# Weight and form preparation in program order, other PSUM banks for the second layer, and another buffer for the transposed tokens

## The chip, the cores and the metric

The kernel runs on one core of a Trainium2 chip. TensorE (PE) multiplies, the vector engine (DVE), ScalarE (ACT) and GpSimd (POOL) work on the elements, and SyncE (SP) and POOL issue DMAs. Matrix results land in PSUM, which has eight banks; everything else lies in SBUF. The metric is the time of one execution on the device, in microseconds, lower is better.

## What is computed

Three layers follow one another on 2304 tokens (4 sequences of 576) of width 512; the reference, shortened:

```python
# 1: attention, 8 heads of 64, causal by blocks of 64
attn = softmax(mask(q @ k.T / 8)) @ v
x = attn.transpose(0, 2, 1, 3).reshape(2304, 512)
# 2: mixture of 8 experts, every token through every expert
P = exp(x @ w_gate - max)
for _ in range(8):
    P /= P.sum(1, keepdims=True); P /= P.sum(0, keepdims=True); P *= N / E
for e in range(8):
    out += P[:, e:e+1] * (relu(x @ w1[e]) @ w2[e])      # w1[e] 512x1024, w2[e] 1024x512
# 3: soft mixture, 8 experts of 4 slots
logits = out @ phi                                       # 2304 x 32
slot_in = softmax(logits, over tokens).T @ out           # 32 x 512
slot_out[e] = relu(slot_in[e] @ m2w1[e]) @ m2w2[e]
result = softmax(logits, over slots) @ slot_out
```

## The kernel before

Every float32 number of the second layer is held as a sum of two rounded halves, high and low, and a product is three matmuls: high x high, high x low, low x high. Products of 2x2 blocks are done with seven block products instead of eight, so there are sums and differences of blocks ("forms") on both sides: of the tokens (T1 to T4, B11, B21, B22), of the first weights (A11, A12, A22, S1 to S4) and of the second ones (B.., T..).

**The main loop** has 13 steps. A step takes two quarters of an expert's 1024 hidden columns ("a" and "b", 256 each) through all tokens, which are three chunks of 768, c = 0, 1, 2. For each chunk there is a first layer (`l1_steps`, matmuls at L880 into banks La, Lb, Lc; ACT copies and relus at L893, L904; DVE additions at L901 and combinations at L898, L912, L953; the splits of the hidden blocks into halves, high on ACT at L908 and low on DVE or POOL at L909) and a second layer (`L2S`, matmuls at L996 into banks l2a and l2c, three token tiles i = 0, 1, 2 at a time, added with the gate's weight into `acc` by DVE at L1003). L1ORD lists the first layer's pieces: the last matmuls are those of product 4, and then come the combinations of quarter a (`af ag ah ai`) and b (`bf bg bh bi`), which read the banks La for the last time. PMAJ lists the second layer: products P1 and P2 for the three tiles, and then the others.

**Preparation.** While a chunk runs, the weights of the next step are prepared, one item at a time: a form (`lin`, POOL, L785), its rounded high half (`hi`, ACT, L790) and the rest (`lo`, DVE, L794), from a raw tile `r` that a DMA has brought (`raw`). `pipe` staggers the three over successive calls, and `pops` and `pop2` call one after each piece of a layer. The ten early items of the first weights (W1E) are called in c = 2's first layer, the four late ones (W1L) in its second; the eight early ones of the second weights (W2E) in c = 0's first layer, the six late ones (W2L) in its second. The forms of the tokens (`forms`, L715 to L723) are built once, ahead of the main loop, in scratch tiles tA and tB.

**The order** on each engine is not the order of these calls. A scheduler lists the instructions by its own estimate of when they can run, and may put a preparation ahead of work that was written before it; each engine then goes through its list strictly in order.

**The last stage.** The last two quarters of the last expert run outside the loop (`L1BE`, `LMAJ`). As tokens are finished, the third layer begins: groups g of four tiles of 128 tokens are transposed (xt, L1185), copied by ACT into a buffer x2a (L1189), multiplied by phi (lg, L1197), and each group is closed with maximum, exponential, two transposes (dT, dR) and a product with the tokens (si, L1243). After the last group comes sit (L1361), and then the slots' two layers (h, sox, soy), whose weights `mw` SP loads in 128 pieces of 256 KB (L1151, L1155). x2a lies in the tile tagged `t4`, which is also the first layer's temporary t (L953).

## Time and profile before

| | us |
|---|---|
| median of three runs (lowest, highest) | 1929.01 (1927.41, 1934.23) |
| the profiled execution | 1932.13 |
| its span | 1930.2 |

Of that span attention and the first expert quarters take the first 450 us, the main loop runs to about 1715, the last quarters to 1832, and the slots' layers from 1870 to the end. PE is the busiest engine. In the profile an engine's row says when an instruction starts, how long it takes and, in brackets, how long the engine stood idle before it and what released it. Matmuls overlap, so that the spacing of their starts, and not their length, is what one costs. PEclk is the clock granted to PE as a share of 2.4 GHz; the other level is 1.2 GHz.

### The profile page before, as it was taken

The numbers are of one execution on the slowest core, as the hardware profiler recorded it, in microseconds if no ns is written. First come the engines' busy times: TensorE is split into PE (matmuls) and PEld (weight loads), VectorE is DVE, ScalarE is ACT, GpSimd is POOL, SyncE is SP. The second block draws the span as 40 slices with busy tenths as digits, with TensorE's granted clock in tenths as the row PEclk, the third lists the DMA queues.
The fourth block names the chain that finished last, engine by engine and source line by source line (L and its number), as shares of the span: only waits on it lengthen the run. The fifth ranks groups of instructions, "written<-read, shape, count | busy, mean of one in ns | idle before, by whom it ended". The sixth has DMA issues, their size and how long they took to land.

```text
span 1930.2 us, 33537 instructions
## 1 busy us (share of the span) xinstructions
PE 1807.6 (94%) x12109; PEld 1662.4 (86%) x12109; DVE 1394.3 (72%) x3154; ACT 908.4 (47%) x2260; POOL 786.1 (41%) x1068
## 2 busy tenths in 40 slices
PE   6999999889999999999999999999999999989987
PEld 4777788778899999999999999898999999989743
DVE  7877767597777777777777787878787878775511
ACT  5667646444535444444454545444444444442313
POOL 6535333444343434343435353535353535342110
PEclk9999999999999999999999999999999999999979
DMA  5544443685746464646464656565655555554759
GB/s 188 168 151 144 135 134 98 198 286 165 223 154 230 156 229 154 225 163 224 164 221 167 215 173 208 180 200 188 191 197 192 196 184 204 178 191 137 248 200 327
DMA packets 145204, 365.98 MB, mean 190 GB/s; under 512 B 12688, under 2 KB 82064, under 8 KB 145040
## 3 DMA queue, kind: packets, MB, share of 16 engines
q0 software_dynamic: 42336, 231.23, 35.7%
q1 hardware_dynamic: 102704, 132.62, 21.1%
q8 instruction: 96, 1.57, 0.3%
q14 instruction: 68, 0.56, 0.1%
HBM read 337.85 MB, written 25.95 MB: 188 GB/s over the span
## 4 chain that ended last, share of the span: by engine, by line
PE 53%; DVE 26%; ACT 8%; DMA 8%; issue 3%; POOL 2%; SPq 0%; ACTq 0%; POOLq 0%; DVEq 0%
PE l2a L996 12%; PE l2c L996 11%; PE La L880 7%; DMA r<-in_moe_w_dram 7%; PE Lb L880 6%; DVE w2f L794 4%; PE l L194 3%; ACT Hxl L893 3%; DVE tA L912 3%; DVE t L953 2%; DVE Hxl L898 2%; DVE tB L912 2%; PE pvp L542 2%; DVE tB L901 2%; DVE Hxh L909 2%
## 5 line engine op out<-in xcount | busy, mean ns | idle before, releaser
L880 PE MATMUL La<-XBT,w1f 128*128 128x384 f32 x1512 | 295.9, 339 | 4.4 <-DVE tB L901 4.4
L1003 DVE SCALAR_TENSOR_TENSOR acc<-l2a,P,acc 128x256 f32<-128x256 f32 x504 | 228.7, 477 | 75.1 <-PE l2a L996 74.6
L996 PE MATMUL l2a<-w2f,Hxl 128*128 128x256 f32 x1512 | 228.6, 288 | 49.4 <-ACT Hxl L908 42.6
L880 PEld LDWEIGHTS La<-XBT,w1f 128*128 128x128 f32 x1512 | 265.5, 188 | 8.7 <-DVE tB L901 8.6
L996 PEld LDWEIGHTS l2a<-w2f,Hxl 128*128 128x128 f32 x1512 | 205.3, 194 | 54.3 <-ACT Hxl L908 46.7
L1003 DVE SCALAR_TENSOR_TENSOR acc<-l2c,P,acc 128x256 f32<-128x256 f32 x378 | 168.4, 478 | 71.1 <-PE l2c L996 68.3
L996 PE MATMUL l2a<-w2f,Hxh 128*128 128x256 f32 x1134 | 191.5, 288 | 0.0
L996 PEld LDWEIGHTS l2a<-w2f,Hxh 128*128 128x128 f32 x1134 | 162.6, 196 | 1.1 <-issue 1.0
L996 PE MATMUL l2c<-w2f,Hxl 128*128 128x256 f32 x756 | 113.0, 297 | 10.8 <-DVE tB L912 10.8
L996 PEld LDWEIGHTS l2c<-w2f,Hxl 128*128 128x128 f32 x756 | 104.1, 203 | 19.2 <-DVE tB L912 19.2
L880 PE MATMUL Lb<-XBT,w1f 128*128 128x384 f32 x504 | 119.9, 360 | 0.0
L785 POOL TENSOR_TENSOR st<-r 128x256 f32<-128x256 f32 x112 | 86.0, 772 | 78.5 <-DMA r<-in_moe_w_dram 45.9
L790 ACT ACTIVATE w1f<-st 128x256 fp32r<-128x256 f32 x112 | 46.2, 413 | 141.0 <-PE Lb L880 119.9
L880 PE MATMUL La<-XBB,w1f 128*128 128x384 f32 x504 | 108.0, 346 | 2.3 <-DVE acc L1003 0.9
L880 PE MATMUL Lb<-XBB,w1f 128*128 128x384 f32 x504 | 102.8, 339 | 0.0
L880 PE MATMUL Lc<-XBB,w1f 128*128 128x384 f32 x504 | 102.5, 338 | 0.0
L996 PE MATMUL l2c<-w2f,Hhx 128*128 128x256 f32 x756 | 96.1, 280 | 0.0
L880 PEld LDWEIGHTS Lb<-XBT,w1f 128*128 128x128 f32 x504 | 95.9, 205 | 0.1
L489 POOL TENSOR_SCALAR pe<-pe,sm 128x384 f32<-128x384 f32 (+2 forms) x80 | 59.3, 744 | 84.2 <-DVE sm L476 43.0
L996 PEld LDWEIGHTS l2c<-w2f,Hhx 128*128 128x128 f32 x756 | 91.7, 188 | 0.8 <-issue 0.8
L880 PEld LDWEIGHTS La<-XBB,w1f 128*128 128x128 f32 x504 | 86.6, 192 | 6.2 <-DVE tA L912 4.5
L909 POOL TENSOR_TENSOR Hhx<-tA,Hhx 128x384 fp32r<-128x384 f32 x42 | 43.1, 1026 | 117.7 <-ACT Hhx L908 117.7
(275 smaller groups left out, 4508.1 us busy)
## 6 DMA issues: line engine op xcount, KB each, us to landing
XBT<-xf0T POOLq DMA_DIRECT2D x56, 768.0 KB, 5.8
XBT<-xf1T POOLq DMA_DIRECT2D x56, 768.0 KB, 7.0
XBT<-xf2T POOLq DMA_DIRECT2D x56, 768.0 KB, 6.1
r<-in_moe_w_dram SPq DMA_DIRECT2D x80, 512.0 KB, 5.9
mw<-in_moe_w_dram SPq DMA_DIRECT2D x128, 256.0 KB, 5.5
XBB<-xf0B POOLq DMA_DIRECT2D x42, 768.0 KB, 6.1
XBB<-xf1B POOLq DMA_DIRECT2D x42, 768.0 KB, 6.9
XBB<-xf2B POOLq DMA_DIRECT2D x42, 768.0 KB, 6.0
```

What stands on the lines that cost most here:

```text
L194: nc.tensor.matmul(o, lh, w[:, kf, :], start=(m == 0), stop=(m == 5))
L489: nc.gpsimd.tensor_scalar(out=p_[:, 0:n_], in0=p_[:, 0:n_], scalar1=sm[:, i:i + 1], scalar2=1.0, op0=ALU.mult, op1=ALU.mult)
L542: nc.tensor.matmul(o[64 * a:64 * a + 64, lo:hi], w, r(a), start=(m == 0), stop=(m == len(its) - 1))
L785: nc.gpsimd.tensor_tensor(out=o, in0=a, in1=b, op=alu)
L790: nc.scalar.activation(out=h, in_=src(), func=AF.Copy)
L794: nc.vector.tensor_tensor(out=lo, in0=src(), in1=f32(h), op=ALU.subtract)
L880: nc.tensor.matmul(o, w[:, i, k], x[:, j, k], start=(first and k == 0 and m == 0), stop=(k == 1 and m == 2), skip_group_check=not first)
L893: nc.scalar.activation(out=o, in_=i, func=AF.Relu)
L909: SLO[nm].tensor_tensor(out=h[:, 1], in0=t, in1=f32(h[:, 0]), op=ALU.subtract)
L912: nc.vector.scalar_tensor_tensor(out=o, in0=a, scalar=0.0, in1=b, op0=ALU.max, op1=op)
L996: nc.tensor.matmul(o, lh, rh, start=(m == 0 and p in ("P1", "P2", "P5")), stop=(m == 5), skip_group_check=p in ("P6", "P3", "P7", "P4"))
L1003: nc.vector.scalar_tensor_tensor(out=av, in0=o, scalar=P[:, t, e:e + 1], in1=av, op0=ALU.mult, op1=ALU.add)
```

## The change

1. `kp` keeps the preparation in the order in which it is written, on POOL, ACT and DVE, for forms and weights alike. `pipe` staggers by one call more (`lo` three calls after `lin`); two loads of the token forms come a call later, and so does the gate's maximum.
2. The late first-weight items and the raw loads of the second weights stand in another order.
3. In the second layer the banks of l2c are (7, 5, 3) instead of (3, 5, 4), and (4, 5, 3) in the last stage.
4. In the last stage c = 0's second layer is written ahead of the third layer's tiles; x2a lies in a free half of the tile H4 instead of `t4`, which becomes a second buffer for the last second layer only.

```diff
--- before.py
+++ after.py
@@ -246,7 +246,7 @@
                 side.append([gate_a(c)])
                 side.append([gate_b(c)] + ([gmax_a] if c == 2 * NCH - 1 else []))
                 if c == 2 * NCH - 1:
-                    side.append([gmax_b])
+                    side.extend([[], [gmax_b]])
                     for r in range(8):
                         side.extend([[] for _ in range(SG)])
                         side.append([col_norm(r == 7)])
@@ -681,16 +681,19 @@
     nst = [0]
     fdn = set()
 
+    def kp(ins):
+        tc.keep_in_program_order(ins)
+
     def pipe(items):
         n = len(items)
 
         def step(t):
             def f():
-                for j, m in ((t - 2, 2), (t - 1, 1), (t, 0)):
+                for j, m in ((t - 3, 2), (t - 2, 1), (t, 0)):
                     if 0 <= j < n and items[j][m] is not None:
                         items[j][m]()
             return f
-        return [step(t) for t in range(n + 2)]
+        return [step(t) for t in range(n + 3)]
 
     SG_T = ["w1f4", "w1f5", "w1f6"]
 
@@ -712,15 +715,15 @@
 
             def lin():
                 q = tmp4(k)
-                nc.gpsimd.tensor_tensor(out=q[o], in0=q[a], in1=q[b], op=alu)
+                kp(nc.gpsimd.tensor_tensor(out=q[o], in0=q[a], in1=q[b], op=alu))
 
             def hi():
                 st[0] = pb.tile([128, 2, HT], F32R, tag=SG_T[nst[0] % 3], name="stg")
                 nst[0] += 1
-                nc.scalar.activation(out=st[0][:, 0], in_=tmp4(k)[o], func=AF.Copy)
+                kp(nc.scalar.activation(out=st[0][:, 0], in_=tmp4(k)[o], func=AF.Copy))
 
             def lo():
-                nc.vector.tensor_tensor(out=st[0][:, 1], in0=tmp4(k)[o], in1=f32(st[0][:, 0]), op=ALU.subtract)
+                kp(nc.vector.tensor_tensor(out=st[0][:, 1], in0=tmp4(k)[o], in1=f32(st[0][:, 0]), op=ALU.subtract))
                 nc.sync.dma_start(out=xf[c, n][:, :, k, :], in_=f32(st[0]))
             return lin, hi, lo
 
@@ -782,16 +785,16 @@
         return st_t[ui][:, 0:256], st_t[ui][:, 256:512]
 
     def pop_(o, a, b, alu):
-        nc.gpsimd.tensor_tensor(out=o, in0=a, in1=b, op=alu)
+        kp(nc.gpsimd.tensor_tensor(out=o, in0=a, in1=b, op=alu))
 
     def prep(dst, src, lin):
         def hi():
             h, lo = dst()
-            nc.scalar.activation(out=h, in_=src(), func=AF.Copy)
+            kp(nc.scalar.activation(out=h, in_=src(), func=AF.Copy))
 
         def lo_():
             h, lo = dst()
-            nc.vector.tensor_tensor(out=lo, in0=src(), in1=f32(h), op=ALU.subtract)
+            kp(nc.vector.tensor_tensor(out=lo, in0=src(), in1=f32(h), op=ALU.subtract))
         return lin, hi, lo_
 
     def items_w1(u, ui):
@@ -847,7 +850,7 @@
         return [it["ab".index(x[0])][x[1:]] for x in names.split()]
 
     W1E = "aA11 aS1 bA11 aS2 bS1 aS4 bS2 aS3 bS4 bS3"
-    W1L = "aA12 bA12 aA22 bA22"
+    W1L = "aA12 aA22 bA12 bA22"
     W2E = "aB11 aT1 bB11 bT1 aB21 aT2 bB21 bT2"
     W2L = "aB22 bB22 aT4 bT4 aT3 bT3"
 
@@ -976,9 +979,9 @@
                 yield o
 
     SEQ = [("P1", "A11", "B11"), ("P2", "A12", "B21"), ("P5", "S1", "T1"), ("P6", "S2", "T2"), ("P3", "S4", "B22"), ("P7", "S3", "T3"), ("P4", "A22", "T4")]
-    ABK, CBK = (2, 1, 0), (3, 5, 4)
-
-    def L2S(c, e, order):
+    ABK, CBK, CBE = (2, 1, 0), (7, 5, 3), (4, 5, 3)
+
+    def L2S(c, e, order, cbk=CBK):
         oa, ob = {}, {}
 
         def prod(p, i, uis):
@@ -986,7 +989,7 @@
             if p == "P1" and 0 in uis:
                 oa[i] = bk(ABK[i], "l2a")[:, 0:256]
             if p in ("P2", "P5") and 0 in uis:
-                ob[i] = bk(CBK[i], "l2c")[:, 0:256]
+                ob[i] = bk(cbk[i], "l2c")[:, 0:256]
             o = ob[i] if p in ("P2", "P5", "P3") else oa[i]
             for ui in uis:
                 m = 3 * ui
@@ -1034,8 +1037,8 @@
         p = list(fo[c][2])
         if c + 1 < NCH:
             nb_, nl = fo[c + 1][0:2]
-            p[6] = lambda f=p[6]: (f(), nl(0))
-            p[9] = lambda f=p[9]: (f(), nl(1), nb_())
+            p[7] = lambda f=p[7]: (f(), nl(0))
+            p[10] = lambda f=p[10]: (f(), nl(1), nb_())
         return p
 
     p1 = fsteps(1)
@@ -1115,7 +1118,9 @@
             if c == 0:
                 l = (pipe(pick(items_w2, u0, W2L)) if s else []) + [raw(1, u0 + 2, 0), raw(1, u0 + 3, 1)]
             elif c == NCH - 1:
-                l = pipe(pick(items_w1, u0 + 2, W1L)) + [raw(2, u0 + 2, 0), raw(2, u0 + 3, 1)]
+                l = pipe(pick(items_w1, u0 + 2, W1L))
+                l[5:5] = [raw(2, u0 + 2, 0)]
+                l.append(raw(2, u0 + 3, 1))
             else:
                 l = []
 
@@ -1131,6 +1136,14 @@
     aux.extend([None] * 4 + pipe(pick(items_w2, u0, W2E)))
     l1_run(L1BE, lambda n: load_x(1, n), lambda j: pops(1))
     drain()
+    l = pipe(pick(items_w2, u0, W2L))
+
+    def pop2(j, x):
+        if j >= 6 and not (6 <= j < 18 and j % 2 == 0) and l:
+            run1(l.pop(0))
+    l2_run(L2S(0, e, PMAL, CBE), pop2)
+    while l:
+        run1(l.pop(0))
     ORD = list(range(12)) + [12, 15, 13, 16, 14, 17]
     wt, wtag = {}, []
     nload = [0]
@@ -1155,7 +1168,6 @@
                     nc.sync.dma_start(out=w[:, i].rearrange("p (k f) -> p k f", k=2), in_=m2w2[e_, r0:r0 + 256, 256 * xy:256 * xy + 256].rearrange("(k p) f -> p k f", p=128))
 
     cc = pb.tile([128, 512], F32, tag="cc", name="cc")
-    x2s = [pb.tile([128, 512], F32, tag="t4", name="x2a")]
     same, mb = cc[:, 0:128], cc[:, 256:384]
     phi_sb = cc[:, 128:256].rearrange("p (k s) -> p k s", k=KD)
     nc.sync.dma_start(out=same, in_=cst[:, 128:256])
@@ -1170,6 +1182,7 @@
     m18 = LVT[:, 968:968 + NT]
     H4 = pb.tile([128, 1024], F32, tag="r2", name="H4")
     nmask = H4[:, 512:640]
+    x2s = [H4[:, 0:512]]
     nc.gpsimd.tensor_scalar(out=nmask, in0=same, scalar1=-1.0, scalar2=-NEG, op0=ALU.add, op1=ALU.mult)
     mo = {}
     nx2 = [0]
@@ -1294,21 +1307,15 @@
         if last:
             load_w([(pb, f"w1f{i}", 2) for i in range(7)] + [(pb, "tB", 3), (pb, "tA0", 1), (pb, "tA1", 1)])
 
-            for p, i in L2S(c, e, [x for x in LMAJ]):
+            x2s.append(pb.tile([128, 512], F32, tag="t4", name="x2a"))
+            for p, i in L2S(c, e, LMAJ, CBE):
                 mpop()
                 if p == "P4":
                     push_t(3 if i < 2 else 4, (2 * i, 2 * i + 1) if i < 2 else (0, 1))
                     if i:
                         push_g(2 + i)
-        else:
-            l = pipe(pick(items_w2, u0, W2L)) if c == 0 else []
-
-            def pop2(j, x):
-                mpop()
-                if j >= 6 and not (6 <= j < 18 and j % 2 == 0) and l:
-                    run1(l.pop(0))
-            l2_run(L2S(c, e, PMAL), pop2)
-            assert not l
+        elif c:
+            l2_run(L2S(c, e, PMAL, CBE), lambda j, x: mpop())
         if c == 0:
             push_t(0, range(4))
             push_g(0)
```

Lines behind the first hunks move down by three (L790 is L793, L794 is L797, L908 is L911), those of the last stage by 13 (L1197 is L1210).

On ACT, around the transition of c = 2 in the first step. Before, with w2f a second-weight tile, Hxh, Hxl and Hhx hidden blocks, r_7740 the raw tile:

```order
L790 ACTIVATE w1f_5724<-st 128x256
L908 ACTIVATE Hxh_5940<-t_4947 128x384
L908 ACTIVATE Hxh_5955<-tB 128x384
L908 ACTIVATE Hhx_5944<-tA_4948 128x384
L790 ACTIVATE w2f_5738<-r_7740 128x256
L908 ACTIVATE Hxh_5955<-tB 128x384
L908 ACTIVATE Hxh_5940<-tA_4949 128x384
L908 ACTIVATE Hxl_5959<-t_4947 128x384
```

The same place now:

```order
L911 ACTIVATE Hxh_5955<-tB 128x384
L793 ACTIVATE w1f_5725<-st 128x256
L911 ACTIVATE Hxh_5940<-t_4947 128x384
L911 ACTIVATE Hxh_5955<-tB 128x384
L911 ACTIVATE Hhx_5944<-tA_4948 128x384
L911 ACTIVATE Hxl_5959<-t_4947 128x384
L911 ACTIVATE Hxh_5940<-tA_4949 128x384
L911 ACTIVATE Hhx_5963<-tB 128x384
L911 ACTIVATE Hxl_5959<-tB 128x384
L793 ACTIVATE w1f_5208<-r_7111 128x256
```

The second-weight item that stood among the splits is gone from here (it comes after the next chunk's first evictions); a first-weight item stands between the first two splits.

On DVE, the end of c = 0's first layer in the second step; L901 (now L904) adds a bank to a tile, L912 (L915) combines, L909 (L912) is a low half, L794 (L797) a preparation. Before:

```order
L953 TENSOR_TENSOR t_4947<-tA_4949 128x384
L909 TENSOR_TENSOR Hhl<-tA_4949,Hhl 128x384
L901 TENSOR_TENSOR tB<-Lc,tB 128x384
L909 TENSOR_TENSOR Hxh_5940<-t_4947,Hxh_5940 128x384
L912 SCALAR_TENSOR_TENSOR tA_4948<-tA_4948,t_4947 128x384
L912 SCALAR_TENSOR_TENSOR tB<-La,tB 128x384
L912 SCALAR_TENSOR_TENSOR tA_4949<-La,tA_4949 128x384
L953 TENSOR_TENSOR t_4947<-tB 128x384
L909 TENSOR_TENSOR Hxh_5955<-tB,Hxh_5955 128x384
L912 SCALAR_TENSOR_TENSOR tB<-tB,t_4947 128x384
L909 TENSOR_TENSOR Hxl_5959<-t_4947,Hxl_5959 128x384
L912 SCALAR_TENSOR_TENSOR tB<-La,tB 128x384
```

And now:

```order
L912 TENSOR_TENSOR Hhl<-tA_4949,Hhl 128x384
L904 TENSOR_TENSOR tB<-Lc,tB 128x384
L797 TENSOR_TENSOR w2f_5739<-r_7730,w2f_5739 128x256
L797 TENSOR_TENSOR w2f_5735<-st,w2f_5735 128x256
L956 TENSOR_TENSOR t_4947<-tA_4949 128x384
L915 SCALAR_TENSOR_TENSOR tB<-La,tB 128x384
L915 SCALAR_TENSOR_TENSOR tA_4948<-tA_4948,t_4947 128x384
L912 TENSOR_TENSOR Hxh_5940<-t_4947,Hxh_5940 128x384
L797 TENSOR_TENSOR w2f_5761<-r_7756,w2f_5761 128x256
L912 TENSOR_TENSOR Hxh_5955<-tB,Hxh_5955 128x384
L956 TENSOR_TENSOR t_4947<-tB 128x384
L915 SCALAR_TENSOR_TENSOR tA_4949<-La,tA_4949 128x384
```

The chain of combinations is the same; three preparations now stand in it, which before were ahead of the first layer's first addition.

On PE, the end of the last second layer (l2a, l2c) with the token steps (xt, lg). Before:

```order
L996 MATMUL l2a<-w2f_5750,Hhh 128x256 x3
L996 MATMUL l2a<-w2f_5772,Hxh_5955 128x256 x3
L1197 MATMUL lg<-x2a,cc 32x128 x4
L1185 MATMUL xt<-ident,acc_2939 128x128 x4
L1197 MATMUL lg<-x2a,cc 32x128 x4
L1185 MATMUL xt<-ident,acc_4145 128x128 x4
L1197 MATMUL lg<-x2a,cc 32x128 x4
L1185 MATMUL xt<-ident,acc_4145 128x128 x4
L1197 MATMUL lg<-x2a,cc 32x128 x4
L1226 MATMUL dT<-ident,LVT 128x128
L1243 MATMUL si<-acc_2939,LVT 32x512 x2
L1243 MATMUL si<-acc_4145,LVT 32x512 x2
```

And now:

```order
L1210 MATMUL lg<-x2a,cc 32x128 x4
L999 MATMUL l2a<-w2f_5747,Hxh_5940 128x256 x3
L999 MATMUL l2a<-w2f_5769,Hxl_5959 128x256 x3
L1198 MATMUL xt<-ident,acc_4908 128x128 x4
L1346 MATMUL mt<-H_19071,ident 128x128
L999 MATMUL l2a<-w2f_5751,Hhh 128x256 x3
L999 MATMUL l2a<-w2f_5773,Hxh_5955 128x256 x3
L1210 MATMUL lg<-H_19071,cc 32x128 x4
L1198 MATMUL xt<-ident,acc_4909 128x128 x4
L1239 MATMUL dT<-ident,H_19071 128x128
L1210 MATMUL lg<-x2a,cc 32x128 x4
L1256 MATMUL si<-acc_4907,LVT 32x512
```

Before, the last second-layer matmuls are followed by ten lg and eight xt of 4 matmuls each, of which the rows show the first ones; now by two lg and one xt.

## Rows read from the trace of the kernel before

**Rows 1.** The page: busy time, share and instructions by engine

```profile
PE 1807.6 (94%) x12109; PEld 1662.4 (86%) x12109; DVE 1394.3 (72%) x3154; ACT 908.4 (47%) x2260; POOL 786.1 (41%) x1068
```

**Rows 2.** PE's waits: what waited for what, us in total, times, longest

```profile
PE l2a L996 <- ACT Hxl L908: 42.6, 13, 3.8
PE l2c L996 <- DVE tB L912: 10.8, 26, 0.4
...
PE l2a L996 <- DVE tB L912: 6.8, 3, 3.1
...
PE gm L297 <- DVE mbg L293: 5.2, 1, 5.2
...
PE La L880 <- DVE tB L901: 4.4, 13, 0.3
```

**Rows 3.** PE's timeline at the first long stall: start, length, instruction, idle, releaser

```profile
525.74 1.15 PE L880 MATMUL La<-XBB,w1f 128*128 128x384 f32 x5
530.20 0.80 PE L996 MATMUL l2a<-w2f,Hxl 128*128 128x256 f32 x2 [3.31 <-ACT Hxl L908]
```

**Rows 4.** ACT's timeline at the same place

```profile
528.49 0.42 ACT L790 ACTIVATE w2f<-r 128x256 fp32r<-128x256 f32 x1 [3.76 <-DMA r<-in_moe_w_dram]
```

**Rows 5.** PE's timeline at three later transitions

```profile
557.85 2.31 PE L996 MATMUL l2a<-w2f,Hxl 128*128 128x256 f32 x18
...
588.36 2.31 PE L996 MATMUL l2a<-w2f,Hxl 128*128 128x256 f32 x18
...
593.90 0.98 PE L996 MATMUL l2c<-w2f,Hxl 128*128 128x256 f32 x6 [0.41 <-DVE tB L912]
...
1697.18 1.28 PE L996 MATMUL l2a<-w2f,Hxl 128*128 128x256 f32 x3 [3.83 <-ACT Hxl L908]
```

**Rows 6.** Windows of one step's chunks: length, busy by engine, PEclk, DMA

```profile
530.20:563.40 33.20, 32.79 (x209) 32.47 (x209) 28.81 (x62) 16.83 (x39) 15.15 (x21) 0.91 0.56 193
563.40:593.90 30.50, 30.09 (x210) 29.77 (x210) 20.75 (x44) 12.16 (x26) 12.45 (x18) 1.00 0.56 182
593.90:628.38 34.48, 30.68 (x212) 29.78 (x212) 25.70 (x54) 15.50 (x37) 13.54 (x18) 1.00 0.58 195
```

**Rows 7.** DVE's timeline behind the first layer of chunk 1

```profile
590.72 1.25 DVE L953 TENSOR_TENSOR t<-tB 128x384 f32<-128x384 f32 x1
...
593.30 0.54 DVE L912 SCALAR_TENSOR_TENSOR tB<-La,tB 128x384 f32<-128x384 f32 x1
```

**Rows 8.** POOL's timeline there

```profile
590.55 1.01 POOL L909 TENSOR_TENSOR Hhx<-tA,Hhx 128x384 fp32r<-128x384 f32 x1 [2.26 <-ACT Hhx L908]
```

**Rows 9.** Line L953: durations in ns, lowest, median, highest

```profile
L953 DVE TENSOR_TENSOR t<-tB x42: 549/1255/1326, 462.0 to 1795.7; 128x384 f32<-128x384 f32 x42
```

**Rows 10.** Line L794, one of its forms, with the same columns

```profile
L794 DVE TENSOR_TENSOR w1f<-st,w1f x112: 407/420/949, 369.4 to 1691.8; 128x256 fp32r<-128x256 f32 x112
```

**Rows 11.** Window of chunk 2's first layer and the long stall

```profile
607.19:628.38 21.19, 17.39 (x108) 16.49 (x106) 15.86 (x32) 13.01 (x32) 7.80 (x12) 1.00 0.85 285
```

**Rows 12.** The tile x2a: its copies

```profile
L1189 ACT ACTIVATE x2a<-xt x18: 597/598/599, 1799.7 to 1861.9; 128x512 f32<-128x512 f32 x18
```

**Rows 13.** PE's timeline around the end of the last second layer

```profile
1818.62 0.66 PE L1185 MATMUL xt<-ident,acc 128*128 128x128 f32 x4
...
1821.01 0.66 PE L1185 MATMUL xt<-ident,acc 128*128 128x128 f32 x4
...
1831.12 0.52 PE L996 MATMUL l2a<-w2f,Hxh 128*128 128x256 f32 x3
...
1855.43 1.12 PE L1185 MATMUL xt<-ident,acc 128*128 128x128 f32 x4
...
1859.14 1.12 PE L1185 MATMUL xt<-ident,acc 128*128 128x128 f32 x4
...
1869.37 0.49 PE L1361 MATMUL sit<-H,A 128*128 128x128 f32 x2 [1.24 <-DVE H L1345]
```

**Rows 14.** The tile mw: issues of the second 64 weight loads

```profile
L1155 SPq DMA_DIRECT2D mw<-in_moe_w_dram x64: 367/368/1124, 1845.8 to 1909.9; - x64
```

## The prediction

> **What bounds the kernel now.** I read the page first: TensorE (PE) is busy for 1807.6 of 1930.2 us, the vector engine (DVE) for 1394.3 [rows 1]. So at most 122.6 us of PE idling are to be won, and whatever the half clock costs beside them. Then PE's waits: the largest group by far is the second layer's start waiting for ACT's split (L908), 42.6 us in 13 pieces; behind it come 26 waits of up to 0.4 us and 3 of up to 3.1 us for DVE's combination into tB (L912) [rows 2]. Thirteen is the number of steps of the main loop, so I looked at one in the timeline: PE ends its first-layer matmuls at 526.89 and starts l2a at 530.20, 3.31 us idle [rows 3]. ACT's timeline says why: a weight preparation (L790, w2f<-r) stands ahead of the remaining splits in ACT's order, and it waited 3.76 us for its DMA [rows 4]. The last step has the same stall, 3.83 us at 1697.18 [rows 5].
>
> The windows by chunk give the price of a step. From the end of one wait at the start of a second layer to the end of the next it is 33.20, 30.50 and 34.48 us with nearly equal matmul counts (209, 210, 212) [rows 6]. The middle one without the 0.41 us wait at 593.90 [rows 5] is 30.09, so three undisturbed chunks are 90.3. A step is (1697.18 - 530.20)/12 = 97.25 us on average [rows 3, 5], so 7.0 us are lost in each: about 4.5 of waits (3.3, two of 0.4, and 0.3 in the first layer [rows 2]), the rest, 2.5, is half clock: the chunk behind the long stall has PE busy for 32.79 us instead of 30.09, at a mean granted clock of 0.91 [rows 6]. Thirteen steps lose 91 us.
>
> **Main loop.** The pinned order puts w2f<-r behind all splits and into the next chunk's first layer. ACT's block goes, and with it up to 3.3 us a step. What is late next is DVE. In the chunk without any preparation (c=1) DVE's last combination ends at 593.84 and PE goes on at 593.90 [rows 5, 7]; PE's second layer had begun, behind the last first-layer matmul, at 588.36 [rows 5], so the first layer takes 5.5 us more on DVE. Against that PE now has, before it needs that bank: P1 and P2 for three token tiles (36 matmuls; 18 of them show 2.31 us with the last one's tail [rows 5], so 0.12 apiece and 4.3 us; none waits for tB any more, since the third tile's bank comes from another chain), and six hoisted matmuls of the next chunk at 0.18 (1.1): 5.4 us of cover. So the 0.41 of c=1 shrinks to about 0.1, and in c=0 and c=2 every microsecond of preparation that falls into that tail is a microsecond of stall. Behind `Lc` the new DVE order has three preparations (L794, now L797) in the tail of c=0 and three in that of c=2: 3 x 0.42 [rows 10] = 1.3, so 1.4 us of stall in c=0, where 0.4 were. In c=2 ten preparations and eight forms of GpSimd (POOL) stand in the stretch, of which DVE was busy for 15.86 of 21.19 us before [rows 11]; for the forms that arrive late I add 0.7 and take 2.1 us, and leave the 0.3 us wait in the first layer. Waits per step: 1.4 + 0.1 + 2.1 + 0.3 = 3.9 instead of 4.5.
>
> The bounds. Below: DVE idles for 5.3 us of c=2's stretch [rows 11], so the preparations might be absorbed, and 0.5 us of waits remain. Above: they displace DVE fully and POOL slows it. Of that the trace shows one thing: L953 (two operands in memory) takes from 0.55 to 1.33 us, and 1.26 as a rule, in the form that reads tB [rows 9]; there it starts 0.2 us after a 1.01 us instruction of POOL [rows 7, 8]. L794 of the same kind has a median of 0.42, but up to 0.95 [rows 10]. If each of eight forms in c=2 and four in c=0 cost one such 0.7, that is 5.6 and 2.8 us more.
>
> By the Trainium skill ("SBUF — State Buffer", section "SBUF: two separate sides") vector instructions with two memory inputs and GpSimd's that read memory hold one port pair by turns, each for its whole length, and the loser stands still. The 1.26 us of L953 agrees. In full the rule would add those 8.4 us (5.6 + 2.8) to each step, and the loop would lose more than in the third rival; the median of L794 speaks for few such meetings, which is what the forecast has.
>
> Half clock: it followed the long stall. At 2.1 and 1.4 us I expect it sometimes and keep a third of 2.5, 0.85 us a step. The loss per step is then 3.9 + 0.85 = 4.75 against 7.0: 2.25 x 13 = **29 us** gained.
>
> **First expert stage (360 to 450 us).** Part of the preparation runs on DVE ahead of the gate's maximum, for which PE waits 5.2 us once [rows 2]. With preparation later this gap can go, and shorter ones like it (up to 12 us with the clock). But the 14 second-layer preparations of the first step now fall into its first chunk's first layer: 14 x 0.42 = 5.9 us, a stall of up to 7. I take +3 (-7 to +12).
>
> **Tail.** Before, the buffer of the transposed tokens is the one that L953 writes, so no copy x2a could run until chunk 2's first layer was over; the first is at 1799.7 [rows 12]. All 18 token steps then follow one another through one buffer. After the last second-layer matmul (1831.6) seven of them, with their group chains, stand bare until sit at 1869.37, 37.7 us [rows 13]. In the new order groups 0 to 2 are transposed inside c=1 and c=2; behind the last second-layer matmul one xt and two lg remain. A step is 2.4 us (1818.62 to 1821.01), at the half clock 3.7 (1855.43 to 1859.14) [rows 13]: three of the one and four of the other, 22 us, with about 4 of a group's chain, leave the tail at about 11.5. PE's work does not go, though: of a step it is about 1.4 us (its first xt to its last lg without the wait between), so 7 x 1.4 + 3 (the si) = 13 us now lie ahead of the second layer's end. Net 37.7 - 11.5 - 13 = 13; c=2's second layer, whose start waited up to 3.1 us [rows 2], should give back some. I take 16. Bounds: nothing, where the last weights set the end: the second 64 loads (256 KB) go out from 1845.8 to 1909.9, 1.0 us apart [rows 14], and if that is their own pace, nothing before them helps. If they only waited for buffers, which now come free earlier, PE alone sets the gain: 13, with the 6.8 us of waits at the last starts [rows 2] and some 4 of half clock back, up to 24.
>
> **Sum.** 1932.13 (the profiled execution; span 1930.2) - 29 - 3 - 16 = 1884. The median of the runs shown is 3.1 below the profiled one, so 1881.
>
> **Rivals.**
> 1. DVE sets the end of each first layer anyway, so the loop keeps its 7.0 us: two stalls near 2 instead of one of 3.3, half clock after each. Only the tail's 16 remain: 1932 - 16 - 3 = 1913. For it: 15.86 us of DVE work in c=2's stretch [rows 11]. Against: three preparations in a tail, not ten.
> 2. The idle time takes the preparations in: waits of 0.5 and no half clock. 6.5 x 13 = 84, cut to 74 for those that meet POOL, with 19 in the tail and 3 at the start: 1932 - 96 - 3 = 1833. For: DVE's 5.3 idle us in c=2. Against: they now stand in the chain, not beside it.
> 3. Slower: POOL's pinned forms delay DVE at both ends, in c=0 and c=2. At half of the 0.7 us price: c=0 2.8, c=2 4.9 + 0.4, half clock after both 5.0, so 13.1 a step; 6.1 x 13 = 79 lost, 16 + 3 won: 1932 + 60 - 3 = 1989. It decides from a loss of 8.5 us a step (7.0 + 19/13). For: the 1.26 us of L953 [rows 9]. Against: L794's median [rows 10].
> 4. The tail is held by the weights' loads: nothing there, 1897; inside the forecast's own range.
>
> **How the numbers follow.** Forecast with rival 4: 0.55 (1862 to 1905); rival 1: 0.20 (1905 to 1925); rival 2: 0.15 (1830 to 1862); rival 3: 0.10, of which 0.02 near no change. What a measurement here can tell from no change is about 0.5%, so "faster" ends at 1919: all of the forecast and of rival 2, 0.18 of rival 1, together 0.88; "same" the other 0.02 with 0.02 of rival 3; slower 0.08. The range, 1842 to 1920, leaves out rival 3 and half of rival 2, and little of rival 1.
>
> **What would show it.** Right: ACT no longer idle for a weight's DMA at c=2's transition; PE waits there for DVE (L915, tB) of 1.5 to 2.5 us, and of 1 to 1.7 in c=0; a step of about 95 us; sit within 13 us of the last second-layer matmul. Wrong: L797 or L956 near 1 us in the tails of c=0 and c=2, a clock below full in two chunks of each step, or splits on ACT that wait behind a late form because the pinned order puts it first.

## The result

The changed kernel takes 1912.18 us in the median of nine runs (1910.84 to 1920.64), the kernel before 1929.63 in nine: a ratio of 0.9916 (0.9899 to 0.9933). It is faster by 17 us, where 48 were forecast (1881). The profiled execution of the changed kernel has a span of 1910.3 us, 19.9 less than before.

To see where they come from I cut both spans at the starts of the second layers, which PE's timeline shows as the first l2a matmul behind a first layer: up to chunk 1 of the first step; from there twelve steps on; and the rest.

| us | before | after | difference | forecast |
|---|---|---|---|---|
| up to the first step's c = 1 | 490.2 | 496.6 | +6.4 | -3 |
| twelve steps | 1167.9 | 1162.3 | -5.6 | -27 (29 for thirteen) |
| the rest | 272.1 | 251.4 | -20.8 | -18 (the last step's 2 and the tail's 16) |
| span | 1930.2 | 1910.3 | -19.9 | -48 |

The last stage did what was forecast, and the loop next to nothing. PE's waits in the changed kernel over the whole run, against those of [rows 2] (columns as there):

```profile
PE La L883 <- DVE tA L915: 27.3, 25, 1.8
PE La L883 <- DVE tB L915: 15.4, 13, 1.3
PE La L883 <- DVE tB L904: 10.4, 14, 1.6
...
PE l2c L999 <- DVE w2f L797: 5.9, 13, 1.1
```

ACT's 42.6 us in 13 pieces are gone; in their place stand four groups of waits, all for DVE. One step of PE's timeline shows them; the first row is c = 2's transition, where [rows 3] had 3.31 us, the others belong to c = 0, which before had one wait of 0.42:

```profile
533.07 2.20 PE L883 MATMUL La<-XBB,w1f 128*128 128x384 f32 x9 [1.75 <-DVE tA L915]
...
558.84 1.31 PE L883 MATMUL La<-XBT,w1f 128*128 128x384 f32 x6 [0.68 <-DVE tB L904]
...
562.12 1.60 PE L999 MATMUL l2c<-w2f,Hxl 128*128 128x256 f32 x12
564.14 0.97 PE L999 MATMUL l2c<-w2f,Hxl 128*128 128x256 f32 x6 [0.41 <-DVE w2f L797]
565.54 1.31 PE L883 MATMUL La<-XBB,w1f 128*128 128x384 f32 x6 [0.43 <-DVE tA L915]
568.10 1.14 PE L883 MATMUL La<-XBB,w1f 128*128 128x384 f32 x5 [1.25 <-DVE tB L915]
```

That is 1.75 + 0.68 + 0.41 + 0.43 + 1.25 = 4.52 us a step, as much as the 4.5 before. In windows (columns as in [rows 6]), a step with the clock at full and one in which it fell, as it did in 4 of the twelve steps:

```profile
533.06:629.32 96.26, 91.54 (x630) 89.10 (x630) 72.92 (x158) 44.16 (x102) 43.08 (x55) 1.00 0.59 194
821.84:919.60 97.76, 93.06 (x630) 90.62 (x630) 72.92 (x158) 44.13 (x102) 43.01 (x55) 0.98 0.59 191
```

And DVE's timeline in c = 0 of the same step, which says what it did while PE waited; the tail begins with the addition of Lc at 560.66:

```profile
557.18 0.80 DVE L797 TENSOR_TENSOR w2f<-st,w2f 128x256 fp32r<-128x256 f32 x1
...
558.24 0.55 DVE L904 TENSOR_TENSOR tB<-La,tB 128x384 f32<-128x384 f32 x1
...
560.66 0.55 DVE L904 TENSOR_TENSOR tB<-Lc,tB 128x384 f32<-128x384 f32 x1
561.12 0.42 DVE L797 TENSOR_TENSOR w2f<-r,w2f 128x256 fp32r<-128x256 f32 x1
561.46 0.42 DVE L797 TENSOR_TENSOR w2f<-st,w2f 128x256 fp32r<-128x256 f32 x1
...
563.66 0.42 DVE L797 TENSOR_TENSOR w2f<-r,w2f 128x256 fp32r<-128x256 f32 x1
563.99 0.56 DVE L912 TENSOR_TENSOR Hxh<-tB,Hxh 128x384 fp32r<-128x384 f32 x1
564.46 0.56 DVE L956 TENSOR_TENSOR t<-tB 128x384 f32<-128x384 f32 x1
...
565.40 0.90 DVE L915 SCALAR_TENSOR_TENSOR tB<-tB,t 128x384 f32<-128x384 f32 x1
566.22 1.36 DVE L912 TENSOR_TENSOR Hxl<-t,Hxl 128x384 fp32r<-128x384 f32 x1
567.50 0.55 DVE L915 SCALAR_TENSOR_TENSOR tB<-La,tB 128x384 f32<-128x384 f32 x1
```

POOL's timeline beside it; L788 (L785 before) makes a form, L912 is a split's low half:

```profile
556.93 0.76 POOL L788 TENSOR_TENSOR st<-st,r 128x256 f32<-128x256 f32 x1
...
563.92 1.96 POOL L912 TENSOR_TENSOR Hhx<-tA,Hhx 128x384 fp32r<-128x384 f32 x1 [2.94 <-ACT Hhx L911]
565.85 1.32 POOL L912 TENSOR_TENSOR Hhh<-tA,Hhh 128x384 fp32r<-128x384 f32 x1
567.12 1.31 POOL L912 TENSOR_TENSOR Hhx<-tB,Hhx 128x384 fp32r<-128x384 f32 x1
```

DVE is not idle anywhere here. Three preparations stand in the chain as forecast, each 0.42 us, and two instructions with both operands in memory take 0.90 and 1.36 us instead of 0.55, beside POOL's splits, as L953 did beside one [rows 7, 8]. Ahead of the chain, the preparation at 557.18 takes 0.80 us beside POOL's form, in this step and in those behind it; then comes the addition for which PE waits 0.68 us.

The tail, in PE's timeline (against [rows 13]): the last second-layer matmul ends at about 1839.3, sit starts at 1845.67, 6.4 us later, where it was 37.7.

```profile
1838.79 0.52 PE L999 MATMUL l2a<-w2f,Hxh 128*128 128x256 f32 x3
1839.24 1.06 PE L1210 MATMUL lg<-H,cc 128*32 128x128 f32 x8
1840.23 0.66 PE L1198 MATMUL xt<-ident,acc 128*128 128x128 f32 x4
...
1845.67 0.49 PE L1368 MATMUL sit<-H,A 128*128 128x128 f32 x2
```

The second 64 weight loads go out from 1844.6 to 1890.0, 0.72 us apart where they were 1.0 [rows 14]: the 1.0 was not their own pace.

```profile
L1168 SPq DMA_DIRECT2D mw<-in_moe_w_dram x64: 367/368/876, 1844.6 to 1890.0; - x64
```

Now the loads themselves hold the end. The chain of work that ended last goes through one weight load after another, nine pieces from 1841.12 to 1894 (first and last shown: start, length); before it went through PE's slot layers until 1904.

```profile
1841.12 6.18 DMA mw<-in_moe_w_dram
...
1888.71 5.44 DMA mw<-in_moe_w_dram
```

PE's last long group of the slots' second layer is paced by them: 0.117 us a matmul now (first row), 0.079 before (second).

```profile
1883.52 12.60 PE L1413 MATMUL soy<-mw,hP 128*32 128x256 f32 x108
```

```profile
1911.49 3.15 PE L1406 MATMUL soy<-mw,hP 128*32 128x256 f32 x40
```

From sit to the end it is 64.6 us, where it was 60.8.

### The profile page after: what moved, and what is told of

Its sections match the earlier page's. It is cut to its first block, busy times and chain, and to the rows that moved or that the text cites. A ratio compares the mean times of both kernels' runs of the same rounds, so it can differ in the third digit from the quotient of the medians.

```text
span 1910.3 us, 33430 instructions
## 1 busy us (share of the span) xinstructions
PE 1793.8 (94%) x12109; PEld 1641.5 (86%) x12109; DVE 1370.0 (72%) x3154; ACT 903.1 (47%) x2260; POOL 804.5 (42%) x1068
## 4 chain that ended last, share of the span: by engine, by line
PE 58%; DVE 27%; DMA 6%; ACT 5%; issue 2%; POOL 1%; SPq 0%; ACTq 0%; DVEq 0%; POOLq 0%
PE l2a L999 15%; PE La L883 11%; PE l2c L999 10%; PE Lb L883 8%; DVE tB L915 3%; DVE Hxl L901 3%; PE l L194 3%; DMA mw<-in_moe_w_dram 3%; DVE Hxh L912 3%; DVE t L956 3%; PE pvp L542 2%; DVE tA L915 2%; DVE tB L904 2%; DVE w2f L797 2%; ACT Hxl L896 2%
## 5 line engine op out<-in xcount | busy, mean ns | idle before, releaser
L883 PE MATMUL La<-XBT,w1f 128*128 128x384 f32 x1512 | 298.3, 339 | 11.8 <-DVE tB L904 10.4
L883 PEld LDWEIGHTS La<-XBT,w1f 128*128 128x128 f32 x1512 | 263.5, 188 | 16.9 <-DVE tB L904 14.9
L999 PE MATMUL l2a<-w2f,Hxl 128*128 128x256 f32 x1512 | 234.0, 286 | 7.1 <-ACT w2f L793 2.3
L999 PE MATMUL l2a<-w2f,Hxh 128*128 128x256 f32 x1134 | 198.6, 289 | 0.8
L999 PEld LDWEIGHTS l2a<-w2f,Hxh 128*128 128x128 f32 x1134 | 167.4, 196 | 7.4 <-ACT w2f L793 3.7
L883 PE MATMUL La<-XBB,w1f 128*128 128x384 f32 x504 | 117.8, 357 | 46.4 <-DVE tA L915 27.3
L883 PEld LDWEIGHTS La<-XBB,w1f 128*128 128x128 f32 x504 | 85.4, 191 | 64.5 <-DVE tA L915 32.5
L907 ACT ACTIVATE tA<-Lb 128x384 f32<-128x384 f32 x42 | 20.6, 490 | 251.8 <-PE Lb L883 251.8
L999 PE MATMUL l2c<-w2f,Hxl 128*128 128x256 f32 x756 | 104.4, 288 | 7.3 <-DVE w2f L797 5.9
L883 PE MATMUL Lb<-XBT,w1f 128*128 128x384 f32 x504 | 104.5, 338 | 3.2 <-DVE tB L915 3.2
L999 PEld LDWEIGHTS l2c<-w2f,Hxl 128*128 128x128 f32 x756 | 96.6, 192 | 11.1 <-DVE w2f L797 8.8
L883 PE MATMUL Lb<-XBB,w1f 128*128 128x384 f32 x504 | 102.0, 338 | 0.0
L907 ACT ACTIVATE tA<-La 128x384 f32<-128x384 f32 x84 | 41.3, 491 | 128.4 <-PE La L883 109.1
L883 PE MATMUL Lc<-XBB,w1f 128*128 128x384 f32 x504 | 101.8, 337 | 0.0
L912 POOL TENSOR_TENSOR Hhx<-tA,Hhx 128x384 fp32r<-128x384 f32 x42 | 54.9, 1308 | 107.2 <-ACT Hhx L911 107.2
L788 POOL TENSOR_TENSOR st<-r 128x256 f32<-128x256 f32 x112 | 89.6, 804 | 24.9 <-DVE w1f L797 22.8
```

Of the source, the lines that this page charges most:

```text
L788: kp(nc.gpsimd.tensor_tensor(out=o, in0=a, in1=b, op=alu))
L883: nc.tensor.matmul(o, w[:, i, k], x[:, j, k], start=(first and k == 0 and m == 0), stop=(k == 1 and m == 2), skip_group_check=not first)
L907: nc.scalar.activation(out=t, in_=o, func=AF.Copy)
L912: SLO[nm].tensor_tensor(out=h[:, 1], in0=t, in1=f32(h[:, 0]), op=ALU.subtract)
L999: nc.tensor.matmul(o, lh, rh, start=(m == 0 and p in ("P1", "P2", "P5")), stop=(m == 5), skip_group_check=p in ("P6", "P3", "P7", "P4"))
```

## Experiments

The theories. A: the pinned preparation took the stall away from ACT in c = 2 and put another one in c = 0, where DVE works through pinned second-weight items inside the first layer's chain. B: the new banks are to blame, since PE's waits are now at the next chunk's La. C: something else, a step's floor, eats what is removed (the clock, restarts). In the table the chunks are means over twelve steps, each from the start of one second layer to the next, and the name says with which chunk's second layer it begins ("c0" holds c = 0's second layer with its waits); "first" is the stretch up to the first step's c = 1. A first layer's waits lie in the column of the chunk ahead of it: c = 0's 0.68 us is in "c2". Times are medians; the ratio is to runs of the kernel before beside each kernel (medians 1926.0 to 1930.5). In e6, e7, e9, e10 and e12 the lines stand six further down than in the change (L797 is L803, L883 is L889, L912 is L918, L915 is L921).

| kernel | first | c0 | c1 | c2 | step | rest | time | ratio (95%) |
|---|---|---|---|---|---|---|---|---|
| before | 490.2 | 30.50 | 31.10 | 35.73 | 97.3 | 272.1 | 1929.6 | 1 |
| the change | 496.6 | 32.88 | 30.26 | 33.72 | 96.9 | 251.4 | 1912.2 | 0.9916 (0.9899, 0.9933) |
| e1 W2E early | 498.6 | 35.43 | 30.20 | 33.60 | 99.2 | 251.6 | 1941.6 | 1.0054 (1.0033, 1.0074) |
| e2 old banks | 493.7 | 32.80 | 30.52 | 32.67 | 96.0 | 252.6 | 1902.8 | 0.9854 (0.9833, 0.9875) |
| e3 banks alone | 491.6 | 30.19 | 30.89 | 35.64 | 96.7 | 270.8 | 1919.7 | 0.9952 (0.9930, 0.9975) |
| e4 last stage alone | 492.3 | 30.50 | 31.10 | 35.49 | 97.1 | 252.7 | 1911.9 | 0.9901 (0.9879, 0.9923) |
| e5 no pin | 491.6 | 30.19 | 30.83 | 35.87 | 96.9 | 250.2 | 1904.0 | 0.9873 (0.9848, 0.9899) |
| e6 order edge | 490.0 | 30.22 | 30.89 | 31.95 | 93.1 | 250.3 | 1860.7 | 0.9651 (0.9624, 0.9678) |
| e7 edge, stagger 3 | 491.1 | 30.19 | 30.84 | 32.62 | 93.7 | 252.5 | 1867.7 | 0.9684 (0.9660, 0.9708) |
| e8 forms pinned | 497.8 | 30.22 | 30.84 | 35.73 | 96.8 | 251.5 | 1912.9 | 0.9920 (0.9896, 0.9943) |
| e9 edge everywhere | 489.7 | 30.23 | 30.89 | 31.95 | 93.1 | 248.9 | 1857.7 | 0.9629 (0.9588, 0.9671) |
| e10 edge, old banks | 491.6 | 30.50 | 31.11 | 31.50 | 93.1 | 251.9 | 1862.2 | 0.9650 (0.9614, 0.9687) |
| e11 weights pinned | 489.8 | 32.89 | 30.24 | 33.84 | 97.0 | 251.1 | 1905.3 | 0.9874 (0.9838, 0.9910) |
| e12 DVE pinned | 494.0 | 35.75 | 31.37 | 31.89 | 99.0 | 249.4 | 1933.9 | 1.0021 (1.0004, 1.0037) |

**e1: the second weights' preparation four calls earlier** (all diffs here are cut to the lines that matter).

```diff
             elif c == 0:
-                aux.extend([None] * 4 + pipe(pick(items_w2, u0, W2E)))
+                aux.extend(pipe(pick(items_w2, u0, W2E)))
```

> The changed kernel, with the four empty calls ahead of the second weights' early preparation (W2E) in c=0's first layer taken away, so that in DVE's order no preparation stands any more behind the addition of Lc (four did). Theory A (the loop's gain was lost in c=0, because the pinned second-weight preparation sits in the tail of its first layer and holds DVE): of the four waits of c=0 (0.68, 0.41, 0.43 and 1.25 us, 2.77 together) about 0.4 remain, a step is 94 us instead of 96.9, 13 steps give 30 us: 1882 us. Theory B (the new banks make PE's order place the next chunk's La matmuls where they must wait, whatever DVE prepares): the waits of c=0 stay near 2.7 and the time at 1912. Theory C (restarts and the half clock eat whatever waits are removed): waits fall, the step stays above 96, time 1905 to 1912.

Missed by 60 us. The 2.77 us of waits at c = 0's transition went, as theory A says: 0.23 is left. But 9 us later PE meets another one, of 3.07 us, and the clock falls in every one of the twelve steps. PE's timeline and ACT's at this place:

```profile
566.53 0.51 PE L999 MATMUL l2a<-w2f,Hxl 128*128 128x256 f32 x2 [0.23 <-ACT Hxl L911]
...
575.52 0.39 PE L999 MATMUL l2a<-w2f,Hxh 128*128 128x256 f32 x1 [3.07 <-ACT w2f L793]
```

```profile
573.50 0.42 ACT L793 ACTIVATE w2f<-st 128x256 fp32r<-128x256 f32 x1 [3.49 <-POOL st L788]
```

ACT waited for a form on POOL, and POOL had six splits (L912, 1.0 to 1.2 us each) ahead of it: the six late second-weight items, still pinned, came too late for a PE that was not held up before. The expectation had looked at one set of pinned items only.

**e2, e3, e4: the parts apart.** e2 is the changed kernel with the banks of before (its edit below); e3 the kernel before with the new banks alone; e4 the kernel before with the last stage's part alone.

```diff
-    ABK, CBK, CBE = (2, 1, 0), (7, 5, 3), (4, 5, 3)
+    ABK, CBK, CBE = (2, 1, 0), (3, 5, 4), (3, 5, 4)
```

> The changed kernel with the l2c banks of before, (3, 5, 4), everywhere. Theory A: the waits of c=0 stay (2.8 us or more, since bank 4 comes back as one more thing to wait for), c=1 gets its 0.41 back: 1912 to 1922 us. Theory B: without the new banks c=0's waits fall towards the 0.42 of before and c=2's stay: 1885 to 1900.

> The kernel before with the new l2c banks alone, (7, 5, 3) in the loop and (4, 5, 3) in the last stage. By the prediction's price (0.42 in c=0 and 0.41 in c=1, each to about 0): 13 x 0.8 = 10 us less, 1919 us, while the 3.3 us wait of c=2 stays. Theory B: other waits, for the bank of La, take their place and the time does not fall: 1927 or more.

> The kernel before with the last stage's part alone (the buffer of the transposed tokens, the order in which c=0's second layer is written); preparation and banks as before. By the traces the stretch behind the loop's last transition fell from 233.0 to 213.5 us; if that part does it alone, 1929.6 - 19.5 = 1910 us, and the whole change gained nothing outside it. If the pinned preparation had a share in the tail, 1915 to 1922.

The last stage alone gives 17.7 us (1911.9), all that the whole change gives; its buffer and its order are not taken apart. The banks alone give 10, as expected, most of it from both chunks (30.50 to 30.19, 31.10 to 30.89, where 0.4 each were priced). Yet in the changed kernel they cost 9: with the old ones c = 2's chunk is 32.67 instead of 33.72, and c = 0's the same (32.80). So B is right that they hurt beside the pins: without them the wait in c = 2 is 1.37 us instead of 1.75, and the clock fell in one of the twelve steps instead of four. Another 2.9 us of the difference lie in the first stretch, and no run says why. B is wrong on c = 0, whose loss stays without the banks. Neither expectation of e2 had its size.

**e5: no pin.**

```diff
     def kp(ins):
-        tc.keep_in_program_order(ins)
+        return ins
```

> The changed kernel without any pin (the stagger, the loads' places, the banks and the last stage as changed). In DVE's order the second weights' preparation is then back at the head of c=0's first layer, none in its tail, and on ACT second-weight items stand among the splits of c=2 again. Theory A (the pins moved the stall from ACT in c=2 to DVE in c=0): c=0's chunk falls from 32.9 to 30.2 us, c=2's rises from 33.2 to 35 or 36, a step stays at 96.5; with the first step's 11 us stall gone, 1900 to 1905 us. Theory C (a step has a floor near 96, by restarts and the clock, whatever is moved): the same step, so the chunks decide: if c=0's stays near 32.9 without pins, A is wrong.

As A expected, in time and in both chunks: c0 30.19, c2 35.87. ACT's wait for a weight's DMA ahead of the remaining splits is back:

```profile
626.78 0.42 ACT L793 ACTIVATE w2f<-r 128x256 fp32r<-128x256 f32 x1 [4.01 <-DMA r<-in_moe_w_dram]
```

The pins take 2.2 us from c = 2's chunk and put 2.7 into c = 0's; on top they cost 5 us in the first stage. So the changed kernel's time is a balance: against e4, the banks, the stagger and the other places of the loads bring 8 us (1904.0 against 1911.9), and the pins take 8 away (1912.2).

**e6 and e7: keep ACT's items behind the splits, and leave the rest free.** An order edge on ACT alone, from the last split of c = 2's first layer to each second-weight item; no instruction waits for a semaphore more than before. e6 has the old stagger and the old places of the raw loads, e7 the changed ones; e7 is e5 with this edge and nothing else. The edit, shortened:

```diff
+    def an(ins):
+        if anc[0] is not None:
+            tc.add_manual_dep(ins.ins, anc[0].ins.name, NoSync)
     def hi():
         h, lo = dst()
-        kp(nc.scalar.activation(out=h, in_=src(), func=AF.Copy))
+        pin(nc.scalar.activation(out=h, in_=src(), func=AF.Copy))   # pin = an for the second weights
     def sp(nm, t):
-        nc.scalar.activation(out=h[:, 0], in_=t, func=AF.Copy)
+        lsp[0] = nc.scalar.activation(out=h[:, 0], in_=t, func=AF.Copy)
     for c in range(NCH):
+        if c == 0:
+            anc[0] = lsp[0]
```

> The kernel before with the new banks and the last stage's part, no pins, old stagger, and one thing more: the ACT items of the second weights may not stand ahead of the last split of c=2's first layer (an order edge to that split, on ACT alone); they are free to run right behind it, and DVE's items are free altogether. Theory A: both stalls are gone at once; c=0's chunk 30.2, c=1's 30.9, c=2's 32 to 33 us, a step of 93 to 94 instead of 96.5 to 97: 13 x 3 = 39 us below the 1902 that banks and last stage give together, 1858 to 1870 us. Theory C: the step stays above 96: 1895 to 1905.

> As the kernel with the order edge on ACT, but with the changed kernel's stagger of three calls and its places of the raw loads (no pins). In DVE's order two first-weight items then stand in c=2's tail, where the other has none. By theory A 2 x 0.42 us more wait in c=2, 13 x 0.8 = 10 us slower than that one: 1868 to 1880. If the earlier raw loads matter more, equal or faster.

Both came in their ranges (e7 to within 0.3 us), and C is refuted: a step falls to 93.1 us. The edge alone, e7 against e5, gains 36 us. e7 is 7 us behind e6 (10 forecast). In its trace two first-weight items stand on DVE in c = 2's tail, but e6 has one there and not none; PE waits 1.38 us in one piece, where e6 has 0.35 and 0.75. Four things differ between the two (stagger, places of the loads, order of the late items, gate's maximum), and they are not taken apart. A window over one step of e6 shows the clock at full (PEclk 1.00) and PE busy for 91.37 of 93.10 us:

```profile
524.60:617.70 93.10, 91.37 (x633) 89.08 (x632) 75.71 (x158) 44.51 (x100) 41.64 (x56) 1.00 0.60 202
```

**e8 and e11: which pins hold up the first stage.** e8 pins the token forms alone, e11 the weights alone.

> The changed kernel with the pins on the token forms alone; the weights' preparation is free. It separates the first stage: by the traces the first second layer began 4.9 us earlier with the pins, and its first chunk took 11.3 us longer. Theory A: the first belongs to the pinned forms, the second to the pinned weights (14 second-weight items in the first chunk's first layer): start at 455, first chunk 30 to 32 us, loop as without pins: 1895 to 1902 us. If the start is 460 again, the gain there came from the weights' pins: 1900 to 1905.

> The changed kernel with the pins on the weights alone, the token forms free. With the forms' pins alone the first second layer began no earlier and its first chunk took 37 us. If the forms' pins are what holds the first stage up: first chunk 30 to 32 us and the loop as in the changed kernel (32.9, 30.2, 33.2): 1900 to 1906 us. If the weights' pins do their share there, the chunk stays over 35: 1908 to 1913.

e8 missed its expectation and e11 met it, so the loss was the other way round. The first stretch is 497.8 us with the forms' pins alone and 489.8 with the weights' alone: it is the pinned forms that hold up what comes behind them (in the order of DVE eleven weight items then stand in the first chunk's first layer, behind its first addition, and none with the weights' pins alone). The early start shows in neither: the first second layer begins at 460.5 and 458.3, at 454.7 with both and 459.7 before. And the forms' pins are not the only way to that loss: in e12 below, with DVE's weight items pinned and the forms free, the chunk behind that start takes 37.5 us, as long as in e8 (37.2).

**e9 and e10: the edge in the last quarters too; the edge with the old banks.**

```diff
     e, u0 = E - 1, NU - 2
+    anc[0] = lsp[0]
     aux.extend([None] * 4 + pipe(pick(items_w2, u0, W2E)))
```

> The version with the order edge on ACT (banks and last stage new, no pins), and the same edge for the last two quarters too, whose second-weight items still stood among the splits of the loop's last chunk: there ACT's wait for the DMA cost PE 4.2 us and the half clock behind it (chunk 37.9 instead of 32.0 us). Theory A: that chunk falls to 32 or 33 us: 5 us off, 1855 to 1857. If the last stage only takes the time back further on: 1860.

> The version with the order edge on ACT in the loop, with the l2c banks of before, (3, 5, 4). The new banks gained 10 us beside the unpinned preparation of before and lost 9 beside the pinned one. If they take a wait for tB away wherever DVE is not held up by preparation, this is slower by 0.4 us each in c=0 and c=1: c=0's chunk 30.5, c=1's 31.1, 13 x 0.6 = 8 us, 1867 to 1871 us. If what they gain depends on the long stall of c=2, no difference: 1860.

e9 is the fastest, 1857.7 us, 0.9629 (0.9588 to 0.9671) of before; against e6 it gains 3 us of the 5 expected. The chunk falls from 37.9 to 35.6 us and not to 32 or 33: of PE's wait of 4.2 us there 0.69 and 1.45 remain. e10, which is e6 with the old banks, ends near its second alternative but not for its reason: the banks matter little once both stalls are gone, since c0 and c1 are 0.3 and 0.2 longer with the old ones, as priced, and c2 is 0.45 shorter, which was not (e6 has waits of 0.35 and 0.75 us there, e10 the second alone); 1862.2 and 1860.7 us are within each other's spread.

**e12: pin DVE's items alone, in e9.**

```diff
-        kp(nc.vector.tensor_tensor(out=lo, in0=src(), in1=f32(h), op=ALU.subtract))
+        tc.keep_in_program_order(nc.vector.tensor_tensor(out=lo, in0=src(), in1=f32(h), op=ALU.subtract))
```

> The fastest version (order edge on ACT everywhere, new banks and last stage), with DVE's preparation alone pinned again: ACT's and POOL's items stay early, DVE's stand in the first layers, two of the eight behind the addition of Lc in c=0 (four in the changed kernel) and one in c=2. It asks whether DVE's items alone make c=0's stall, or ACT's and POOL's late ones do. If DVE alone: c=0's chunk rises from 30.2 by 2 x 0.42 us for the tail and up to 0.7 for the wait inside the first layer, to 31 to 31.8 us, c=2's by about 0.4; a step 94 to 95, 1870 to 1882 us. If ACT's or POOL's lateness is what counted: chunks 30.2, 30.9, 32.0 as before, 1858 to 1862.

DVE's pins alone make the stall, and a worse one: 76 us, c = 0's chunk 35.75. The expectation had 12 to 24 us, and no fall of the clock, which now comes in every step. PE's timeline, then DVE's and POOL's at the place, and behind them ACT's:

```profile
565.66 0.69 PE L889 MATMUL La<-XBT,w1f 128*128 128x384 f32 x1 [2.91 <-ACT tA L913]
```

```profile
562.04 1.36 DVE L918 TENSOR_TENSOR Hxh<-tB,Hxh 128x384 fp32r<-128x384 f32 x1
563.33 1.34 DVE L921 SCALAR_TENSOR_TENSOR tB<-tB,t 128x384 f32<-128x384 f32 x1
564.60 1.34 DVE L918 TENSOR_TENSOR Hxl<-t,Hxl 128x384 fp32r<-128x384 f32 x1
565.86 0.55 DVE L921 SCALAR_TENSOR_TENSOR tB<-La,tB 128x384 f32<-128x384 f32 x1
```

```profile
561.68 1.32 POOL L918 TENSOR_TENSOR Hhh<-tA,Hhh 128x384 fp32r<-128x384 f32 x1
562.96 1.30 POOL L918 TENSOR_TENSOR Hxh<-tA,Hxh 128x384 fp32r<-128x384 f32 x1
564.22 1.31 POOL L918 TENSOR_TENSOR Hxh<-tB,Hxh 128x384 fp32r<-128x384 f32 x1
```

Two preparations (0.84 us) had delayed the tail until it met POOL's five splits: three DVE instructions take 1.35 us instead of 0.55, and POOL's 1.31 instead of 1.01. POOL's order has changed with DVE's, though no edit names it: three of those splits (Hhh, Hxh, Hxh) stand ahead of Hhx<-tB, behind which they are in e9 and in the kernel before, so that POOL no longer waits between them. In the changed kernel Hhh has moved ahead in the same way. The run does not separate the delay on DVE from this order. PE's next-chunk matmul waits for ACT to empty its bank (L913), and that stands in ACT's order behind a split which waited 2.02 us for DVE's tB, the one written from 563.33 on:

```profile
564.71 0.52 ACT L917 ACTIVATE Hhx<-tB 128x384 fp32r<-128x384 f32 x1 [2.02 <-DVE tB L921]
565.13 0.47 ACT L913 ACTIVATE tA<-La 128x384 f32<-128x384 f32 x1
```

## Why the prediction was wrong

The direction and the range held; the size did not, and the step that failed is the loop's term, "2.25 x 13 = 29 us", where the runs show 0.46 x 12 = 5.6. Of the 1.8 us a step that are missing 0.6 are waits, put too low in c = 0, and 1.2 the rest, which I took for half clock.

- *ACT's block goes*: right, with the waits of c = 1. In c = 2 PE waits 1.75 us, where 2.1 and 0.3 were forecast.
- *"3 x 0.42 [rows 10] = 1.3, so 1.4 us of stall in c=0"*: wrong, 2.77 were measured. I counted the items behind the addition of Lc and no others. The waits at that chain's end, 0.43 and 1.25, are 1.68 and near the forecast, the chain meeting POOL's splits (+0.35 and +0.8). The other 1.09 I had at nothing: the items ahead made PE wait inside the first layer (0.68), and one item was itself what PE needed (0.41). The prediction had the price of a meeting in the rows, but tied it to POOL's forms; in the tail it is POOL's splits that the chain runs into, and L797 takes 0.42 there. One form does cost: 0.38 us of L797's 0.80 at 557.18, ahead of the wait of 0.68. e12 shows that pinning DVE's items is enough to make a stall in c = 0, e5 and e6 that without pins its chunk is 30.2.
- *"keep a third of 2.5, 0.85 us a step"* for the clock: mis-sized, since the 2.5 was not all clock. The fall of the clock itself is 97.76 - 96.26 = 1.5 us in 4 of 12 steps, 0.5 a step, less than the 0.85. But a step at the full clock still takes 96.26. Three chunks without a visible wait, as c = 1 has them now, are 3 x 30.26 = 90.8, with the 4.52 of waits 95.3: about 1.0 us is left. A wait can cost more than its idle time: twelve matmuls from 562.12 at 0.12 us would let the next begin at 563.56, it began at 564.14, 0.58 later, and the row shows 0.41. Some 0.2 us for each of five waits is that 1.0 (an estimate from this one place), and it does not go when one long wait becomes several short ones.
- *The waits' sum* came out at 4.5, not 3.9, and the rest at 2.0 instead of 0.85: 6.6 us lost a step, where 4.75 were forecast and 7.0 before. That is rival 1 (1913), which named the mechanism: DVE sets the end of each first layer. Its half clock behind each stall came in 4 of 12 steps only, and that its total is met within 1 us is in part luck: the first stage lost 6.4 where it has nothing, and the tail gave more than its 16.
- *First stage*, a gain of 3 forecast, a loss of 6.4 measured: inside the bounds given, but the sign was wrong. The first second layer started 4.9 us earlier, and PE's wait of 5.2 us for the gate's maximum is gone, as hoped; the chunk behind it was 11.3 longer, at a mean granted clock of 0.84, where a stall of up to 7 was named. The forms' pins alone make a loss of that size (e8, e11).
- *Tail*, 16 forecast: the total is right, and e4 has it alone with 17.7 in the median. Its parts were not: the bare tail fell by 31.3 us and not 26 (to 6.4, not 11.5), the second layer's end moved 6.8 us back against the start of its stretch (the last step's gain included) and not 13, and 3.8 us were lost behind sit, where I had nothing. Rival 4 is refuted as it stood, since its 1.0 us a load was not the loads' own pace; but at 0.72 us they set the end now, which may cap what a faster last stage can still give.

By the Trainium skill ("SBUF — State Buffer", section "SBUF: two separate sides") a vector instruction with two SBUF inputs and a GpSimd instruction that reads SBUF take one port pair in turn, each for its whole length, and the other stands still. e12's rows agree in kind: DVE instructions with two memory operands and POOL's take 1.34 and 1.31 us when they stand against each other, while the one that reads PSUM beside them keeps 0.55. The turn is shorter than the rule would make it: DVE's start 1.27 us apart, and the two lengths alone, 0.55 and 1.01, add up to 1.56. As a price for every form that passes by, this was rightly left out; as a price for a delayed tail it was wrongly left out.

What stays open: why the new banks add a wait of 0.35 us in c = 2 in e6, and nothing that shows in e3; and how the clock chooses the steps in which it falls. Behind the longest wait of a step it fell in all twelve steps of the kernel before (2.7 to 3.7 us) and of e12 (2.9), in four of the change (1.75) and in none of e6 (0.75) and e7 (1.4).

## What to carry to other kernels

Where one badly placed instruction blocks an engine, move that one: an order edge on one engine gained 36 us (e7 against e5), where pins on all items and three engines traded one stall for another and lost 8 (the change against e5). Work that is pinned into a dependent chain costs its length and whatever the delayed chain then runs into, so look up what each neighbour does half a microsecond later, and whether its own order has changed too. And cut both spans into stages before explaining a total: here the last stage gave all the gain, and the others cancelled.

## What the runs showed of the hardware

DVE instructions with two operands in SBUF and POOL's splits slow each other, both at once, where they stand back to back: in e12 DVE's went from 0.55 to 1.34 us and POOL's from 1.01 to 1.31. In a single meeting one loses and the other runs as alone, and it can be either: before, DVE's L953 took 1.25 us beside a split of 1.01 [rows 7, 8], while in the changed kernel the split at 563.92 took 1.96 and DVE's two beside it 0.56 each.

A wait of PE can cost more than the idle time that its row shows: 0.58 us for 0.41 at 564.14 in the changed kernel.
